# A masked attention without its empty quarter: 64x64 tiles for scores and values in a retention and feed-forward kernel

## The chip, the cores and the metric

The kernel runs on one NeuronCore of one Trainium2 chip. The metric is the time of one execution on the device, in microseconds (us). The profile is one execution of the program taken by the hardware profiler. TensorE (PE, with its weight loads PEld), VectorE (DVE), ScalarE (ACT), GpSimd (POOL) and SyncE (SP) are the engines; all loads and stores are issued on SP's queue.

## What is computed

For each batch and head, a decaying state collects the outer products of keys and values, and each query reads it. The result, all heads of a token side by side, goes through a feed-forward block with a rational function.

```python
batch, n_heads, seq, head_dim = (4, 8, 768, 64)
gamma = 1.0 - 2.0 ** (-5.0 - np.arange(H))
for t in range(S):
    state = gamma * state + outer(k[:, :, t], v[:, :, t])      # per batch and head, 64x64
    y[:, :, t] = scale * (q[:, :, t] @ state)
x = y.transpose(0, 2, 1, 3).reshape(B * S, H * D)              # 3072 tokens x 512
h = x @ w_in                                                   # 512 -> 2048
g = (a0 + a1*h + a2*h**2 + a3*h**3) / (1 + |b0|*|h| + |b1|*h**2 + 1e-6)
out = g @ w_out                                                # 2048 -> 512
```

## The kernel before

**Chunks.** Each sequence of 768 tokens is cut into C = 6 chunks of 128, so there are 24 chunks, numbered 0 to 23; chunk i is number i % 6 of its sequence. For a chunk the state of the tokens ahead is read (`recall`), and the tokens of the chunk itself attend to each other under a causal mask. All of this is fp32.

- `scores` (L220): k times q for all 8 heads into two PSUM banks `pa`. A head is h = 4a + 2r + j with a, r, j in 0, 1; r says in which half of the 128 partitions the 64 dimensions of the head lie in `qT` and `kT`. Each matmul has 64 rows, 128 keys and 128 queries, and the two values of r take the upper and the lower half of the array.
- `mask` (L231): VectorE multiplies each bank by the causal mask into `aT`, two instructions of 128x512.
- `outer` (L239): k times v over the 128 tokens, the new part of the state (`pk`), in the second half of bank `px[1]`. Not done for the last chunk of a sequence.
- `recall` (L252): state times q into `px`; 64 rows and 64 columns a matmul, so four fit in the array. Not done for the first chunk of a sequence.
- `values` (L266): v times `aT` over 128 keys for 128 queries, 64 columns a matmul, added into `px`.
- `update`, `x_out`: VectorE adds `pk` to the state, scales `px`, and splits the result into two fp32r parts `xh` and `xl` (ScalarE and VectorE). `scale_state` and `scale_v` put the decay on state and v and run on GpSimd.

**Feed-forward.** Four chunks make a block of 512 tokens; there are six blocks. For each block and each of 16 slices of the inner dimension `gemm_in` (12 matmuls of 128x512 fp32r, L355) writes a bank `ph`; ScalarE, GpSimd and VectorE work out the rational function (L366 to L395), and `gemm_out` (12 matmuls, L410) comes LAG = 3 slots later. A slot is one such slice.

**Order of the work.** The order on TensorE, VectorE, ScalarE, GpSimd and SP is that of the code: there is no scheduler. `opening` does chunks 0 to 3. Then `run` goes through 96 slots; the attention of chunk 4 and after is laid between the slots by the table `parts`: part 0 of a chunk is its scores and mask, part 1 the rest. In a slot with part 1 TensorE does gemm_in, then outer, recall, values, then gemm_out. The weights come as raw words and are decoded in the first 25 slots or so (`decode_read`, `decode_join`, `decode_split`, `decode_rest`); the banks that these use rotate with `pa` and `px`.

**Loads.** kT of a chunk is loaded two chunks ahead in part 0, and qT, v and k in part 1 (`load_rest`, L197). Chunks 2 and 3 land in buffers that the feed-forward uses later (`borrowed`, L180).

## Time and profile before

| | before |
|---|---|
| timed runs, median of 3 (lowest, highest) | 644.6 us (644.24, 645.17) |
| profiled execution, first to last instruction (span) | 642.4 us |
| TensorE busy | 620.0 us, 97% |
| VectorE, ScalarE, GpSimd busy | 460.1, 441.7, 334.1 us |
| matmuls | 3739 |
| mean DMA rate | 82 GB/s, 52.36 MB in all |

The page gives no time of its own for the profiled execution but its span; the timed runs are 2.2 us longer, which lies before the first and after the last instruction. A row of the views names the line of the code, the engine, the operation, what it writes and reads, its shape, and how many instructions stand in it; the time in square brackets is how long the engine sat idle ahead of it, and what ended that.

### The profile page before, as it was taken

How to read it: one execution, taken by the hardware profiler on the slowest of the kernel's cores; microseconds unless marked ns; L12 is line 12 of the kernel's file. 1: busy time of each engine (PE TensorE's matmuls, PEld its weight loads, DVE VectorE, ACT ScalarE, POOL GpSimd, SP SyncE). 2: the span in 40 equal slices, each digit the busy share in tenths (PEclk: the TensorE clock that was granted, in tenths of full speed). 3: DMA queues.
4: the chain of work that ended last, by engine and by line, in shares of the span. 5: the costliest groups of instructions: out<-in, count | busy, mean ns of one | idle time of the engine just before them, and what ended most of it. 6: DMA issues, size and time to landing. Idle time of an engine off the chain costs nothing.

```text
span 642.4 us, 10022 instructions
## 1 busy us (share of the span) xinstructions
PE 620.0 (97%) x3739; PEld 498.2 (78%) x3742; DVE 460.1 (72%) x731; ACT 441.7 (69%) x721; POOL 334.1 (52%) x288
## 2 busy tenths in 40 slices
PE   8777999999999999999999999999999999999997
PEld 5555778888877778788888878878888888888885
DVE  3788788888888666767676676667766766666664
ACT  2687889889885556566656575766666666777773
POOL 2566668887874434444544453535354434444442
PEclk9988999999999999999999999999999999999999
DMA  8984572001033222310110321001311000010001
GB/s 316 400 331 167 201 252 109 1 1 65 1 121 127 66 67 82 132 51 17 49 50 17 115 51 50 34 21 54 108 33 35 1 0 1 26 41 2 1 1 65
DMA packets 24384, 52.36 MB, mean 82 GB/s; under 512 B 3088, under 2 KB 3216, under 8 KB 24336
## 3 DMA queue, kind: packets, MB, share of 16 engines
q1 hardware_dynamic: 24336, 51.73, 23.4%
q8 instruction: 29, 0.48, 0.3%
q14 instruction: 19, 0.16, 0.1%
HBM read 43.33 MB, written 8.39 MB: 81 GB/s over the span
## 4 chain that ended last, share of the span: by engine, by line
PE 85%; DMA 4%; ACT 4%; DVE 3%; issue 2%; SPq 1%; POOL 0%; POOLq 0%; DVEq 0%; ACTq 0%
PE ph L355 38%; PE po L410 38%; PE px L271 3%; PE pa L226 3%; DMA v<-in_v 1%; PE px L260 1%; PE px L247 1%; DMA qT<-in_qT 1%; DMA k<-in_k 1%; DMA xdec_sb<-in_xdec 1%; ACT s L372 1%; SPq L192 1%; DVE o L428 1%; ACT t L128 1%; ACT q L366 1%
## 5 line engine op out<-in xcount | busy, mean ns | idle before, releaser
L373 POOL TENSOR_TENSOR q<-q,s 128x512 f32<-128x512 f32 x96 | 124.3, 1295 | 228.0 <-ACT s L372 217.9
L355 PE MATMUL ph<-xh,w 128*128 128x512 f32 (+2 forms) x776 | 210.3, 393 | 8.4 <-DVE p L389 4.8
L410 PE MATMUL po<-w,gh 128*128 128x512 f32 x768 | 200.2, 393 | 0.0
L355 PEld LDWEIGHTS ph<-xh,w 128*128 128x128 f32 x776 | 143.9, 188 | 41.5 <-DVE t L147 2.8
L410 PEld LDWEIGHTS po<-w,gh 128*128 128x128 f32 x768 | 142.9, 188 | 32.4 <-ACT p L374 1.5
L366 ACT ACTIVATE q<-ph 128x512 f32<-128x512 f32 x96 | 57.2, 596 | 118.6 <-PE ph L355 118.5
L378 DVE TENSOR_TENSOR p<-ph,p 128x512 f32<-128x512 f32 x96 | 66.2, 690 | 94.3 <-ACT p L374 94.3
L395 POOL TENSOR_TENSOR gl<-p,gh 128x512 fp32r<-128x512 f32 x96 | 124.3, 1295 | 8.9 <-ACT gh L394 3.6
L410 PE MATMUL po<-w,gl 128*128 128x512 f32 x384 | 110.5, 389 | 0.2 <-POOL gl L395 0.2
L387 DVE SCALAR_TENSOR_TENSOR q<-q,qcon,ph 128x512 f32<-128x512 f32 x96 | 71.4, 744 | 47.0 <-ACT ph L384 46.8
L355 PE MATMUL ph<-xl,w 128*128 128x512 f32 (+2 forms) x388 | 103.9, 390 | 0.0
L383 ACT ACTIVATE s<-q,qcon 128x512 f32<-128x512 f32 x96 | 69.4, 722 | 22.5 <-POOL q L373 22.5
L355 PEld LDWEIGHTS ph<-xl,w 128*128 128x128 f32 x388 | 72.8, 188 | 15.3
L410 PEld LDWEIGHTS po<-w,gl 128*128 128x128 f32 x384 | 72.1, 188 | 15.6 <-POOL gl L395 0.6
L379 DVE SCALAR_TENSOR_TENSOR p<-p,par_sb,ph 128x512 f32<-128x512 f32 x96 | 71.8, 748 | 3.4
L374 ACT ACTIVATE p<-ph,par_sb 128x512 f32<-128x512 f32 x96 | 73.1, 761 | 0.0
L388 DVE SCALAR_TENSOR_TENSOR ph<-p,par_sb,ph 128x512 f32<-128x512 f32 x96 | 72.0, 750 | 0.0
L394 ACT CAST gh<-p 128x512 fp32r<-128x512 f32 x96 | 58.8, 613 | 15.9 <-DVE p L389 15.9
L389 DVE SCALAR_TENSOR_TENSOR p<-q,ph 128x512 f32<-128x512 f32 x96 | 65.9, 687 | 3.3
L372 ACT ACTIVATE s<-q,babs 128x512 f32<-128x512 f32 x80 | 65.3, 817 | 2.7
L384 ACT ACTIVATE ph<-s 128x512 f32<-128x512 f32 x96 | 57.8, 602 | 10.0 <-DVE p L379 0.8
L210 POOL TENSOR_TENSOR v<-v,vdec_sb 128x512 f32<-128x512 f32 x24 | 25.0, 1044 | 43.9 <-DMA v<-in_v 43.9
(37 smaller groups left out, 446.2 us busy)
## 6 DMA issues: line engine op xcount, KB each, us to landing
raw<-in_w_in SPq DMA_DIRECT2D x16, 512.0 KB, 5.4
raw<-in_w_out SPq DMA_DIRECT2D x16, 512.0 KB, 7.4
kT<-in_kT SPq DMA_DIRECT2D x24, 256.0 KB, 2.8
qT<-in_qT SPq DMA_DIRECT2D x24, 256.0 KB, 3.0
v<-in_v SPq DMA_DIRECT2D x24, 256.0 KB, 3.5
out<-o SPq DMA_DIRECT2D x24, 256.0 KB, 2.2
k<-in_k SPq DMA_DIRECT2D x20, 256.0 KB, 3.7
half<-o SPq DMA_DIRECT2D x8, 256.0 KB, 2.2
```

Of the source, the lines that this page charges most:

```text
L355: nc.tensor.matmul(ph[:, t0:t1], w1[f][:, part, kt * P : (kt + 1) * P], x[:, kt, t0:t1], start=(i == 0), stop=(i == 3 * NP - 1),)
L372: nc.scalar.activation(s, q, AF.Identity, bias=babs[:, 0:1], scale=babs[:, 1:2])
L373: nc.gpsimd.tensor_mul(q, q, s)
L374: nc.scalar.activation(p, ph, AF.Identity, bias=par_sb[:, 2:3], scale=par_sb[:, 3:4])
L378: nc.vector.tensor_mul(p, ph, p)
L379: nc.vector.scalar_tensor_tensor(p, p, par_sb[:, 1:2], ph, ALU.add, ALU.mult)
L383: nc.scalar.activation(s, q, AF.Abs_reciprocal_sqrt, bias=qcon[:, 0:1])
L387: nc.vector.scalar_tensor_tensor(q, q, qcon[:, 0:1], ph, ALU.add, ALU.mult)
L388: nc.vector.scalar_tensor_tensor(ph, p, par_sb[:, 0:1], ph, ALU.add, ALU.mult)
L389: nc.vector.scalar_tensor_tensor(p, q, 2.0, ph, ALU.subtract, ALU.mult, reverse0=True)
L395: nc.gpsimd.tensor_sub(gl, p, gh.bitcast(F32))
L410: nc.tensor.matmul(o_tiles[n][tt], g_[:, tt * P : (tt + 1) * P], w2[f][:, part], start=(first and m == 0), stop=(last and m == 2),)
```

## The change

In a causal mask over 128 keys and 128 queries, the quarter of late keys (64 to 127) with early queries (0 to 63) is zero. The changed kernel leaves that quarter out.

- **Scores** are sixteen matmuls instead of eight, each with 64 rows and 64 keys: the early keys of a head with all 128 queries, its late keys with the 64 late queries. Each takes a quarter of the array (64x64). For half of the heads (a = 1) the halves of the partitions are exchanged in `qT` and `kT` (`crossed`), and for the heads with r = 1 early and late tokens are exchanged in `k` and `v` (`by_token`), so that all four quarters have work and two heads share 192 columns of a bank: 64 early queries of both, 64 late ones of each.
- **Mask**: two instructions of 128x384 instead of 128x512; the mask in memory has 192 columns instead of 128.
- **Values** come in two groups: `values_early` (64 early keys, 64 early queries, 64x64 tiles) and `values_late` (128 keys, 64 late queries, 128x64 tiles). Eight matmuls each.
- **Recall** keeps its eight matmuls; since q of the heads with a = 1 is exchanged, it reads these from a further load `q2T`, 128x256 (128 KB), for every chunk that is not the first of its sequence: 20 loads more on SP's queue.
- **Order**: in `run` outer now comes last, behind the late values; in `opening` it stays first.
- **Small things**: seven constants share one tile `small`, the zeros of the opening lie in a buffer of `o`, and the borrowed buffers have one shape.

TensorE at the scores of chunk 7, before (names: `pa` the banks written, `ph` and `po` the feed-forward's):

```order
L410 MATMUL po<-w,gh 128x512 x8
L410 MATMUL po<-w,gl 128x512 x4
L226 MATMUL pa<-qT,kT 128x128 x8
L355 MATMUL ph<-xh,w 128x512 x4
L355 MATMUL ph<-xl,w 128x512 x4
```

And after, the same place; 64x2x64 is a matmul of 128 queries that writes two separate blocks of 64 columns:

```order
L447 MATMUL po<-w,gl 128x512 x4
L254 MATMUL pa<-qT,kT 64x128
L254 MATMUL pa<-qT,kT 64x2x64
L254 MATMUL pa<-qT,kT 64x64 x4
L254 MATMUL pa<-qT,kT 64x2x64
L254 MATMUL pa<-qT,kT 64x128 x2
L254 MATMUL pa<-qT,kT 64x2x64
L254 MATMUL pa<-qT,kT 64x64 x4
L254 MATMUL pa<-qT,kT 64x2x64
L254 MATMUL pa<-qT,kT 64x128
L392 MATMUL ph<-xh,w 128x512 x4
```

Eight matmuls of 128 columns became eight of 128 and eight of 64, with half the keys each. Part 1 of the same chunk on TensorE, before (L247 outer, L260 recall, L271 values):

```order
L355 MATMUL ph<-xh,w 128x512 x4
L247 MATMUL px<-v,k 64x64 x8
L260 MATMUL px<-qT,state 64x128 x8
L271 MATMUL px<-aT,v 64x128 x8
L410 MATMUL po<-w,gh 128x512 x8
```

After (L287 recall, L297 early values, L308 late values, L274 outer):

```order
L392 MATMUL ph<-xh,w 128x512 x4
L287 MATMUL px<-qT,state 64x128 x4
L287 MATMUL px<-q2T,state 64x128 x4
L297 MATMUL px<-aT,v 64x64 x8
L308 MATMUL px<-aT,v 64x64 x8
L274 MATMUL px<-v,k 64x64 x8
L447 MATMUL po<-w,gh 128x512 x8
```

Outer moved from the first place to the last, and values became two groups of half the columns. SP's queue at part 1 of chunk 12, where the loads of chunk 14 stand behind the stores of a block, before:

```order
L434 DMA out<-o 128x512 x4
L192 DMA qT<-in_qT 128x512
L192 DMA v<-in_v 128x512
L192 DMA k<-in_k 128x512
L192 DMA kT<-in_kT 128x512
```

And after:

```order
L471 DMA out<-o 128x512 x4
L195 DMA qT<-in_qT 128x512
L195 DMA q2T<-in_q2T 128x256
L195 DMA v<-in_v 128x512
L195 DMA k<-in_k 128x512
L195 DMA kT<-in_kT 128x512
```

v and k now stand behind one more load. The core of the diff:

```diff
 def load_rest(i):
     load_part(i, "qT", qT, 1, [P, NP, P])
+    if i % C > 0:
+        load_part(i, "q2T", q2T, 4, [P, 2, P])
     load_part(i, "v", v, 3, [P, H, D])
...
 def scores(i):
-    for aj in range(NP):
-        for r in range(2):
-            rows = slice(r * D, (r + 1) * D)
-            nc.tensor.matmul(
-                pa[r][:, aj], st["kT"][rows, aj], st["qT"][rows, aj], start=True, stop=True
-            )
+    pa = [bank("pa")[:, : 6 * D].rearrange("p (j t) -> p j t", t=3 * D) for _ in range(2)]
+    for j in range(2):
+        for a in range(2):
+            whole, part = [], []
+            for s in range(2):
+                r = s ^ a
+                kt, qt = (st[n][half(s), 2 * a + j] for n in ("kT", "qT"))
+                to = pa[s][half(r), j, : 3 * D if a != s else 2 * D]
+                if a != s:
+                    to = to.rearrange("p (x t) -> p x t", t=D)[:, ::2]
+                    qt = qt.rearrange("p (x t) -> p x t", t=D)
+                whole.append((to, kt[:, :D], qt))
+                qt = st["qT"][half(s), 2 * a + j]
+                part.append((pa[s][half(1 - r), j, later(a, s)], kt[:, D:], qt[:, D:]))
+            for to, kt, qt in part + whole if a else whole + part:
+                nc.tensor.matmul(to, kt, qt, start=True, stop=True, skip_group_check=True)
...
+def values_early(i):
+    for a in range(2):
+        for j in range(2):
+            for r in range(2):
+                nc.tensor.matmul(
+                    st["px"][r][half(j), a * P : a * P + D],
+                    st["v"][half(r), 4 * a + 2 * r + j], st["aT", r ^ a][half(r), j, :D],
+                    start=(c == 0), stop=(c == 0), skip_group_check=True,
+                )
+def values_late(i):
+    for a in range(2):
+        for r in range(2):
+            for j in range(2):
+                nc.tensor.matmul(
+                    st["px"][r][half(j), a * P + D : (a + 1) * P],
+                    st["v"][:, 4 * a + 2 * r + j], st["aT", r ^ a][:, j, later(a, r ^ a)],
+                    start=(c == 0), stop=(c == 0 or a == 1), skip_group_check=True,
+                )
...
 if part == 1:
-    outer(chunk)
-    recall(chunk)
-    values(chunk)
+    recall(chunk)
+    values_early(chunk)
+    values_late(chunk)
+    outer(chunk)
```

## The prediction

> **What bounds the kernel now.** I read the page first, then the windows by stage, then TensorE's order of time inside one chunk, then the waits.

> ```profile
> PE 620.0 (97%) x3739; PEld 498.2 (78%) x3742; DVE 460.1 (72%) x731; ACT 441.7 (69%) x721; POOL 334.1 (52%) x288
> ...
> PE 85%; DMA 4%; ACT 4%; DVE 3%; issue 2%; SPq 1%; POOL 0%; POOLq 0%; DVEq 0%; ACTq 0%
> ```

> TensorE is busy for 97% of the span and is 85% of the chain that ended last. The windows (length, then busy time of each engine, the granted clock, the DMA share and GB/s) say where this holds:

> ```profile
> 0.00:24.00 24.00, 19.74 (x255) 13.17 (x258) 13.70 (x31) 8.69 (x17) 8.60 (x13) 1.00 0.92 342
> 24.00:57.50 33.50, 22.59 (x177) 17.35 (x173) 27.33 (x47) 27.08 (x47) 20.87 (x19) 0.91 0.76 289
> 57.50:95.00 37.50, 36.62 (x244) 29.42 (x243) 30.85 (x53) 29.81 (x53) 22.90 (x21) 0.99 0.66 222
> 245.00:540.00 295.00, 293.69 (x1801) 237.23 (x1800) 201.80 (x322) 190.32 (x304) 133.41 (x112) 1.00 0.16 49
> ```

> Up to 24 us the loads bound it (DMA share 0.92), up to 57.5 us VectorE and ScalarE with the decoding of the weights; behind that TensorE has under 1 us idle in 37.5 and 1.3 in 295. Chunks 0 to 3 lie in the first stretch, 4 and 5 in the second. So TensorE time counts for chunks 6 to 23, 18 of the 24.

> **The price of a pass.** Chunk 10 on TensorE, in order of time (start, busy us, group):

> ```profile
> 213.71 1.16 PE L226 MATMUL pa<-qT,kT 64*128 64x128 f32 x16
> 214.80 1.19 PE L355 MATMUL ph<-xh,w 128*128 128x512 f32 x4
> ...
> 217.75 0.69 PE L247 MATMUL px<-v,k 128*64 128x64 f32 x16
> 218.36 0.67 PE L260 MATMUL px<-qT,state 64*64 64x128 f32 x16
> 218.96 1.09 PE L271 MATMUL px<-aT,v 128*64 128x128 f32 x16
> 219.98 2.11 PE L410 MATMUL po<-w,gh 128*128 128x512 f32 x8
> ```

> Eight matmuls of the program stand as sixteen, so an fp32 matmul is two passes. From start to start the groups take: scores (L226) 1.09, outer (L247) 0.61, recall (L260) 0.60, values (L271) 1.02 us. Their medians:

> ```profile
> L247 PE MATMUL px<-v,k x320: 221/222/369, 7.6 to 507.9; 128*64 128x64 f32 x160
> L260 PE MATMUL px<-qT,state x320: 269/269/473, 12.9 to 533.4; 64*64 64x128 f32 x160
> L271 PE MATMUL px<-aT,v x384: 272/273/474, 8.7 to 534.4; 128*64 128x128 f32 x192
> ```

> A group's busy time less its last matmul is the time from first to last start: 1.09 - 0.27 = 0.82 us for values, 0.69 - 0.22 = 0.47 for outer. Both run two at a time, in the two column halves, so these are 7 steps each, and 64 columns more cost 0.35/7 = 0.05 a step. As much I put to the first weight load, which nothing covers: a step of 128 columns is (0.82 - 0.05)/7 = 0.11 us, one of 64 is 0.06. I take 0.1095 and 0.059. Over its 8 steps a group then has 0.14 (0.61 - 8 x 0.059) or 0.15 us (1.02 - 8 x 0.1095), for the change of the tile size. Recall has four tiles of 64x64 at work: 4 rounds of 0.1095 leave 0.16 of its 0.60, the same. With nothing put to the weight load the steps would be 0.117 and 0.067 and the change 0.08, and a middle chunk below would gain 0.25, not 0.31.

> **The group of part 1.** Middle chunks have all three groups, 2.23 us (217.75 to 219.98). Now recall and early values share the 64x64 size, late values and outer the 128x64 size: one tile change fewer, and the early keys of the late queries stay while the late keys of the early ones go. Recall 4 x 0.1095 = 0.44, early values 4 rounds of 64 columns 0.24, change 0.155, late values 8 x 0.059 = 0.47, outer 0.47, change 0.15: 1.92 us, 0.31 less. The first and the last chunk of a sequence:

> ```profile
> 232.41 0.67 PE L260 MATMUL px<-qT,state 64*64 64x128 f32 x16
> ...
> 234.03 0.50 PE L410 MATMUL po<-w,gh 128*128 128x512 f32 x1
> ```
> ```profile
> 252.36 0.69 PE L247 MATMUL px<-v,k 128*64 128x64 f32 x16
> ...
> 253.85 0.73 PE L410 MATMUL po<-w,gh 128*128 128x512 f32 x2
> ```

> Last (no outer): 1.62 before; 0.44 + 0.24 + 0.155 + 0.47 + 0.15 = 1.45 after, 0.17 less. First (no recall): 1.49 before, 0.24 + 0.155 + 0.47 + 0.47 + 0.15 = 1.48 after: it loses a quarter of its values and gains a tile change. Chunks 6 to 23 hold 12 middle, 3 last and 3 first ones: 12 x 0.31 + 3 x 0.17 + 3 x 0.01 = 4.3 us.

> **Scores.** Before, 8 steps of 128 columns in two row halves, 1.09 us. Now sixteen matmuls on four tiles: each tile gets long, short, long, short (or short first), 128 and 64 queries. No row shows unequal matmuls side by side; the bounds are recall's and outer's steps. If each tile runs its own list, a tile takes 2 x (2 x 0.1095 + 2 x 0.059) = 0.67, and with 0.155 the group is 0.83 us, 0.26 less. If matmuls may only start in program order, a tile waits for its turn behind a long one twice: the last starts at 0.56 and the group is 0.56 + 0.22 + 0.155 = 0.93, 0.16 less. I take 0.83, by this row, the first round of a recall:

> ```profile
> 188.42 0.34 PE L260 MATMUL px<-qT,state 64*64 64x128 f32 x4
> ```

> Four passes of 0.27 us or more lie within 0.34, so they started within 0.07, less than a step: the next tile's matmul did not wait for the second pass of the one ahead. [...]

> **Where the shorter scores do not count.** Waits of TensorE at part 1 that are not its own:

> ```profile
> 70.61 0.69 PE L247 MATMUL px<-v,k 128*64 128x64 f32 x16 [0.44 <-PE ph L355]
> ...
> 187.81 0.69 PE L247 MATMUL px<-v,k 128*64 128x64 f32 x16 [0.53 <-PE ph L355]
> ...
> 203.08 0.69 PE L247 MATMUL px<-v,k 128*64 128x64 f32 x16 [0.54 <-DVE aT L235]
> ```
> ```profile
> 69.83 0.69 DVE L147 SCALAR_TENSOR_TENSOR t<-raw,u 128x512 uint32<-128x512 uint32 x1
> ...
> 199.35 2.48 DVE L428 TENSOR_TENSOR o<-po,o 128x512 f32<-128x512 f32 x4
> 201.75 1.28 DVE L235 TENSOR_TENSOR aT<-pa,causal_sb 128x512 f32<-128x512 f32 x2
> ```

> At 70.61 the px bank came free with the decode that ended at 70.52; chunks 6, 7 and 8 (187.81) have this wait, and a shorter scores group only lengthens it. Chunk 9 (203.08) waits for its mask, which stood behind four adds. There the mask's own length counts: 1.28 us for two of 512 columns, against 0.75 for two of 256 here:

> ```profile
> 221.39 0.42 DVE L284 TENSOR_TENSOR state<-px,state 128x256 f32<-128x256 f32 x1
> 221.72 0.75 DVE L294 TENSOR_TENSOR px<-px,xdec_sb 128x256 f32<-128x256 f32 x2
> ```

> 384 columns lie halfway, 1.02: 0.26 gained once; elsewhere the mask is off the path. The first of these rows also says what outer's last place costs: VectorE takes up the state's sum at 221.39, 1.4 us after the group's end at 219.98, so it does not wait for outer.

> **The extra loads.** q2T, 128 KB, stands on SP's queue between qT and v, so v (then k, and later loads) is late, and GpSimd's scaling of v holds up its next product:

> ```profile
> 264.47 1.04 POOL L210 TENSOR_TENSOR v<-v,vdec_sb 128x512 f32<-128x512 f32 x1 [4.97 <-DMA v<-in_v]
> 265.48 1.28 POOL L373 TENSOR_TENSOR q<-q,s 128x512 f32<-128x512 f32 x1
> ```
> ```profile
> 270.44 0.74 PE L355 MATMUL ph<-xh,w 128*128 128x512 f32 x2 [1.11 <-DVE p L389]
> ```

> This chain ends in TensorE's 1.11 us at 270.44; its v (chunk 14) comes behind four stores. What 128 KB take goes by the fullest of the page's 40 slices:

> ```profile
> GB/s 316 400 331 167 201 252 109 1 1 65 1 121 127 66 67 82 132 51 17 49 50 17 115 51 50 34 21 54 108 33 35 1 0 1 26 41 2 1 1 65
> ```

> At 400 GB/s they are 0.33 us, so the wait grows by 0.33, and chunk 13's shorter scores, which stand ahead of that wait, are lost in it. Bounds: 0 (the loads before it are late anyway) to 1.8, which the issue ahead of v took once:

> ```profile
> 258.89 1.83 SPq L192 DMA_DIRECT2D qT<-in_qT  x1
> ```

> Chunk 22's v is the other one behind stores with a q2T:

> ```profile
> 466.43 1.04 POOL L210 TENSOR_TENSOR v<-v,vdec_sb 128x512 f32<-128x512 f32 x1 [3.01 <-DMA v<-in_v]
> ```
> ```profile
> 456.35 0.69 PE L247 MATMUL px<-v,k 128*64 128x64 f32 x16
> ```

> It comes 10 us behind its part 1, chunk 14's 12 (252.36 to 264.47), and TensorE has no gap after it; 0.33 us more is covered. At the other loads GpSimd idles afterwards.

> In the opening the q2T of chunks 1 to 3 and 32 KB of mask are 416 KB, 1.06 us at that rate, ahead of v of chunk 3. Its values move from 24.08 to about 25.1 us at their end:

> ```profile
> 23.06 1.09 PE L271 MATMUL px<-aT,v 128*64 128x128 f32 x16
> 24.08 0.97 PE L355 MATMUL ph<-xh,w 128*128 128x384 f32 x4
> ```
> ```profile
> 24.89 0.42 DVE L284 TENSOR_TENSOR state<-px,state 128x256 f32<-128x256 f32 x1
> ```

> VectorE takes them up at 24.89, so 0.8 of it was slack: with qT of chunk 3 late too, but shorter masks, I get 0.35 us, bounds 0 and 1.06. Chunk 5 gives it back: its recall and values took 2.96 us (54.53 to 57.49), at half clock,

> ```profile
> 54.53 1.13 PE L260 MATMUL px<-qT,state 64*64 64x128 f32 x14 [1.72 <-DVE t L147]
> ...
> 57.49 0.71 PE L410 MATMUL po<-w,gh 128*128 128x512 f32 x1
> ```

> and save 2 x 0.17. I set the opening at nothing. The constants in one tile and the zeros in a store's buffer move no instruction.

> **Sum.** Part 1: 4.3. Scores of 13 chunks (18 less 6, 7, 8, 9, 13) x 0.26 = 3.4. Mask of chunk 9: 0.26. Chunk 14's load: -0.33. Together 7.6 us. The profiled span of 642.4 becomes 634.8; the three timed runs have a median of 644.6, 2.2 us more than that span, so I forecast 637.0. A change of 0.2% (1.3 us) is about what can be told from none here.

> **Rivals.** (a) Starts in program order: scores save 0.16, 1.3 us less: 638.3. The first round of recall speaks against it.
> (b) The late v costs more: 1.8 us at chunk 14, and at chunk 22 some 0.7, where v would pass from 10 to 12 us after its part 1: 637.0 + 1.5 + 0.7 = 639.2. For it: the 1.83 us issue; against it: it fell once on these three loads.
> (c) A floor for the issue of passes over all tiles. No group before goes faster than recall's 0.44/16 = 0.027 us a pass; early values would need 0.015, scores 0.021. At 0.027 early values take 0.44, not 0.24, and scores 0.86 + 0.155 = 1.02. Middle chunks then save 0.11, last ones lose 0.03, first ones lose 0.19, scores save 0.07: 1.3 - 0.1 - 0.6 + 0.9 - 0.1 = 1.4 us, 643.2. Against it: the four starts above, at most 0.07/3 = 0.023 apart. [...]
> (d) Slower: unequal matmuls are dealt out in rounds, and each of the four rounds of scores empties the array, 0.155 us, before the next: 4 x (0.22 + 0.155) = 1.50 us, 0.41 more than before. Over 18 chunks that is 7.4, against 4.3 from part 1: 647.7. It decides from a scores group of 1.33 us on (4.3/18 = 0.24 above 1.09). Recall's equal rounds follow each other with no such gap, which speaks against it.

> **Chances.** Likeliest case 0.55, (a) 0.16, (b) 0.12, (c) 0.12, (d) 0.05. The range takes in the likeliest case with its bounds (all 18 scores counted and no late v: 1.7 us better), (a) and (b), and leaves out (c) and (d), 0.17: 635.0 to 640.5. Faster by over 0.2%: the first three and half of (c), 0.88; within: 0.07; slower: 0.05.

> **What would show it.** Right: scores start to start 0.83, the middle group 1.92, late values and outer with no gap between them, TensorE busy some 7 to 8 us less, 0.44 to 0.8 us waits ahead of part 1 in chunks 6 to 8 and under 0.3 in chunk 9. Scores of 0.93 would be (a), of 1.02 with early values at 0.44 (c), of over 1.3 (d); a gap of over 2 us after chunk 14's load (b). It would be wrong above all if short matmuls on four tiles cost more than recall's and outer's steps.

## The result and the profile after

The changed kernel takes 639.9 us (median of four runs, 639.1 to 641.4) against 644.4 us for before (four runs, with the profiled one); the ratio is 0.9926 (95% interval 0.9909 to 0.9943). The forecast was 637.0 us, in a range of 635.0 to 640.5. The profiled execution has a span of 638.0 us, where 634.8 was forecast. Two executions that ran several times slower throughout are left out of all figures: one of before, of 1564.6 us, timed beside e12, and the profiled one of e11, of 3420.8 us.

Two rows of its page, busy time by engine and the chain that ended last:

```profile
PE 611.7 (96%) x4506; PEld 494.4 (77%) x4510; DVE 452.9 (71%) x731; ACT 441.4 (69%) x721; POOL 334.2 (52%) x288
...
PE 67%; ACT 13%; DVE 11%; issue 5%; DMA 2%; POOL 1%; SPq 1%; POOLq 0%; DVEq 0%; ACTq 0%
```

TensorE is busy 8.3 us less, yet ScalarE and VectorE now hold 24% of the chain, where they held 7%. More than half of this lies between 80 and 200 us, where TensorE is busy for 119.3 of the 120 us (119.0 before): the chain runs beside a busy TensorE there, and shows no new limit. To see where time was gained and lost, cut both spans at the same places of the program, which are the first product of the first layer, the scores of chunk 6 and chunk 23's recall, and by the clock at 245 us. Windows of before, then of after (length, busy PE, PEld, DVE, ACT, POOL, granted clock, DMA share, GB/s):

```profile
0.00:24.08 24.08, 19.82 (x255) 13.17 (x258) 13.78 (x31) 8.69 (x17) 8.60 (x13) 1.00 0.92 343
24.08:66.07 41.99, 31.08 (x211) 24.23 (x209) 32.86 (x57) 32.85 (x58) 25.30 (x22) 0.92 0.72 269
66.07:245.00 178.93, 176.83 (x1045) 142.60 (x1045) 148.40 (x235) 140.54 (x237) 122.02 (x107) 1.00 0.27 90
245.00:532.97 287.97, 286.66 (x1746) 231.47 (x1744) 196.26 (x312) 185.83 (x296) 130.85 (x110) 1.00 0.16 50
```
```profile
0.00:26.11 26.11, 19.08 (x382) 12.66 (x386) 12.68 (x31) 8.63 (x17) 8.71 (x14) 0.93 0.94 340
26.11:69.45 43.34, 31.24 (x276) 24.91 (x273) 32.68 (x57) 32.83 (x58) 25.16 (x22) 0.88 0.72 266
69.45:245.00 175.55, 173.97 (x1250) 140.61 (x1249) 145.37 (x233) 139.78 (x236) 121.42 (x107) 1.00 0.28 96
245.00:528.55 283.55, 281.97 (x2105) 229.47 (x2101) 193.38 (x314) 186.44 (x298) 131.58 (x111) 1.00 0.18 55
```

From chunk 6's scores to chunk 23's recall before takes 466.90 us and after 459.10: **7.8 us gained**, and 7.6 was the forecast of the whole sum. Ahead of chunk 6's scores after is **3.4 us late** (69.45 against 66.07), 2.0 of them already at the first product, where the opening was set at nothing.

The gain is where it was forecast. Chunk 10 of after, on TensorE in order of time:

```profile
215.85 0.90 PE L254 MATMUL pa<-qT,kT 64*64 64x128 f32 x32
216.68 1.20 PE L392 MATMUL ph<-xh,w 128*128 128x512 f32 x4
...
219.62 0.45 PE L287 MATMUL px<-qT,state 64*64 64x128 f32 x8
219.89 0.40 PE L287 MATMUL px<-q2T,state 64*64 64x128 f32 x8
220.11 0.41 PE L297 MATMUL px<-aT,v 64*64 64x64 f32 x16
220.45 0.69 PE L308 MATMUL px<-aT,v 128*64 128x64 f32 x16
220.97 0.64 PE L274 MATMUL px<-v,k 128*64 128x64 f32 x16
221.53 2.11 PE L447 MATMUL po<-w,gh 128*128 128x512 f32 x8
```

Scores 0.83 us from start to start (1.09 before), part 1 1.91 (2.23 before). A last and a first chunk, 1.44 (1.62) and 1.48 us (1.49):

```profile
233.69 0.45 PE L287 MATMUL px<-qT,state 64*64 64x128 f32 x8
...
235.13 1.20 PE L447 MATMUL po<-w,gh 128*128 128x512 f32 x4
```
```profile
253.36 0.46 PE L297 MATMUL px<-aT,v 64*64 64x64 f32 x16
...
254.84 0.73 PE L447 MATMUL po<-w,gh 128*128 128x512 f32 x2
```

In the opening, chunk 2's scores and outer product, which came at 15.06 and 16.25 us before; then GpSimd's scaling of its v; then three windows:

```profile
15.48 0.89 PE L254 MATMUL pa<-qT,kT 64*64 64x128 f32 x31
16.71 0.32 PE L254 MATMUL pa<-qT,kT 64*64 64x128 f32 x1 [0.34 <-issue]
18.30 0.93 PE L274 MATMUL px<-v,k 128*64 128x64 f32 x16 [1.26 <-DVE px L329]
```
```profile
17.20 1.04 POOL L218 TENSOR_TENSOR v<-v,small 128x512 f32<-128x512 f32 x1 [3.97 <-DMA v<-in_v]
```
```profile
52.70:56.10 3.40, 0.40 (x2) 0.19 (x2) 2.38 (x4) 3.27 (x7) 2.98 (x3) 1.00 0.00 1
56.10:59.50 3.40, 2.60 (x47) 2.37 (x47) 3.30 (x5) 1.84 (x4) 1.28 (x1) 0.50 0.25 47
59.50:62.93 3.43, 3.43 (x9) 2.75 (x9) 2.69 (x6) 3.40 (x8) 2.96 (x3) 0.50 0.80 265
```

The 1.26 us at 18.30 is put down to VectorE, but the outer product reads v, whose scaling ends at 18.2; that v landed 2.05 us later than before. The stop of 0.34 us ahead of it ("issue") is over by then, so it is the late v that holds the outer product up here. And behind TensorE's waits at 52 to 57 us the clock is halved twice in a row, where before it was halved once (54.5 to 58.0); the second time it falls on the second layer's first product.

### The profile page after: what moved, and what is told of

It reads as the page before. It is cut to its first block, busy times and chain, and to the rows that moved or that the text cites. A ratio compares the mean times of both kernels' runs of the same rounds, so it can differ in the third digit from the quotient of the medians.

```text
span 638.0 us, 11577 instructions
## 1 busy us (share of the span) xinstructions
PE 611.7 (96%) x4506; PEld 494.4 (77%) x4510; DVE 452.9 (71%) x731; ACT 441.4 (69%) x721; POOL 334.2 (52%) x288
## 3 DMA queue, kind: packets, MB, share of 16 engines
q1 hardware_dynamic: 27216, 54.38, 25.1%
## 4 chain that ended last, share of the span: by engine, by line
PE 67%; ACT 13%; DVE 11%; issue 5%; DMA 2%; POOL 1%; SPq 1%; POOLq 0%; DVEq 0%; ACTq 0%
PE po L447 30%; PE ph L392 30%; ACT t L130 3%; ACT s L420 2%; ACT ph L421 2%; DVE q L424 2%; PE pa L254 2%; DVE p L426 2%; DVE ph L425 2%; PE px L308 2%; DMA v<-in_v 2%; PE px L287 2%; PE px L274 1%; ACT u L138 1%; ACT s L409 1%
## 5 line engine op out<-in xcount | busy, mean ns | idle before, releaser
L410 POOL TENSOR_TENSOR q<-q,s 128x512 f32<-128x512 f32 x96 | 124.4, 1296 | 224.1 <-ACT s L409 215.4
L424 DVE SCALAR_TENSOR_TENSOR q<-q,small,ph 128x512 f32<-128x512 f32 x96 | 71.4, 744 | 47.3 <-ACT ph L421 47.2
L420 ACT ACTIVATE s<-q,small 128x512 f32<-128x512 f32 x96 | 69.4, 723 | 22.7 <-POOL q L410 22.7
L416 DVE SCALAR_TENSOR_TENSOR p<-p,small,ph 128x512 f32<-128x512 f32 x96 | 71.8, 748 | 3.4
L411 ACT ACTIVATE p<-ph,small 128x512 f32<-128x512 f32 x96 | 73.2, 762 | 0.0
L425 DVE SCALAR_TENSOR_TENSOR ph<-p,small,ph 128x512 f32<-128x512 f32 x96 | 72.0, 750 | 0.0
L409 ACT ACTIVATE s<-q,small 128x512 f32<-128x512 f32 x80 | 65.3, 816 | 2.7
L218 POOL TENSOR_TENSOR v<-v,small 128x512 f32<-128x512 f32 x24 | 25.0, 1044 | 41.8 <-DMA v<-in_v 40.1
```

Of the source, the lines that this page charges most:

```text
L409: nc.scalar.activation(s, q, AF.Identity, bias=babs[:, 0:1], scale=babs[:, 1:2])
L410: nc.gpsimd.tensor_mul(q, q, s)
L411: nc.scalar.activation(p, ph, AF.Identity, bias=par_sb[:, 2:3], scale=par_sb[:, 3:4])
L416: nc.vector.scalar_tensor_tensor(p, p, par_sb[:, 1:2], ph, ALU.add, ALU.mult)
L420: nc.scalar.activation(s, q, AF.Abs_reciprocal_sqrt, bias=qcon[:, 0:1])
L424: nc.vector.scalar_tensor_tensor(q, q, qcon[:, 0:1], ph, ALU.add, ALU.mult)
```

## The experiments

**Is it the loads? (e1, e2, e3)** First the changed kernel again (e1). In e2 the q2T loads of chunks 1 to 5 are left out:

```diff
-        if i % C > 0:
+        if i % C > 0 and i >= SPB + 2:
             load_part(i, "q2T", q2T, 4, [P, 2, P])
...
-    qt = st["q2T"][half(r), j] if a else st["qT"][half(r), j]
+    qt = st["q2T"][half(r), j] if a and "q2T" in st else st["qT"][half(r), 2 * a + j]
```

> The changed kernel once more, as the measure for the others of this set. The first traces say: behind chunk 6's scores it gains 7.8 us (7.6 forecast), ahead of them it loses 3.4 us. Theory A (the late q2T loads leave TensorE idle in the opening, and the clock is halved once more for it): the loss returns in each run, 639.5 to 641.5 us, and half-clock windows stand near 18 to 22 and 56 to 63 us. Theory B (the windows fall by chance, whatever the kernel): the time scatters over 636.5 to 641 us, and a profile shows other windows than the first.

Measured: 639.2 us (638.6 to 640.1), ratio to before 0.9906 (0.9886 to 0.9926). Chunk 6's scores start at 69.44 us again, and from there to chunk 23's recall (527.92) it gains 8.4 us. The half clock of 56 us is there (55.6 to 62.4), the one of 18.6 us stands elsewhere (7.8 to 14.7): the loss returns, the places of the windows only in part. TensorE's rows of chunk 2 have no stop in the scores this time:

```profile
17.37 0.90 PE L254 MATMUL pa<-qT,kT 64*64 64x128 f32 x32 [0.20 <-DMA qT<-in_qT]
19.42 0.69 PE L274 MATMUL px<-v,k 128*64 128x64 f32 x16 [1.14 <-POOL v L218]
```

The outer product is 3.2 us later than before's (16.25) all the same. The rows above wait for the loads of qT and v.

> No q2T is loaded for chunks 1 to 5; their recall reads the same rows of qT for the four exchanged heads, so that the instructions stay and these heads' recall is not the reference's. Theory A: v of chunk 2 lands 1 us or more earlier, the window near 18 to 22 us is gone, chunk 6's scores start within 1.5 us of before's 66.07 us, and the time is 2 to 3 us under the changed kernel's, 637 to 638 us. Rival (the loss comes from the changed matmul groups or masks in the opening, not from the loads): chunk 6's scores stay 3 us late, and the time stays within 0.7 us of the changed kernel's.

Measured: 637.2 us (635.8 to 639.8), ratio 0.9879 (0.9848 to 0.9910), which overlaps e1's. In the profiled run, the slowest of the four, v of chunk 2 lands 0.7 us earlier than after's, at 16.44, and chunk 6's scores still start at 69.53. Theory A would not have that, though the time, 2.0 us under e1's, is the one it gave (637 to 638), so the run does not decide between the two. TensorE's rows of chunk 2, then its weight loads, show why the profile is late without q2T:

```profile
17.83 0.89 PE L254 MATMUL pa<-qT,kT 64*64 64x128 f32 x31
19.94 0.32 PE L254 MATMUL pa<-qT,kT 64*64 64x128 f32 x1 [1.22 <-issue]
20.19 0.69 PE L274 MATMUL px<-v,k 128*64 128x64 f32 x16
```
```profile
17.83 0.75 PEld L254 LDWEIGHTS pa<-qT,kT 64*64 64x64 f32 x31
19.94 0.13 PEld L254 LDWEIGHTS pa<-qT,kT 64*64 64x64 f32 x1 [1.36 <-issue]
```

Weight loads and matmuls both stop ahead of the last pass of the scores, and nothing is awaited ("issue"). It is the stop of 16.71 us above, but longer. Neither theory had it, and e12 takes it up.

In e3 the kernel before gets the loads alone:

```diff
         load_part(i, "qT", qT, 1, [P, NP, P])
+        if i < NSTEP and i % C > 0:
+            nc.sync.dma_start(out=st["q2T"], in_=qT[i // C, i % C][:, 2:])
         load_part(i, "v", v, 3, [P, H, D])
```

> The kernel before with one thing added: the second half of each qT is loaded once more behind qT, into a tile that nothing reads (the zeros lie in a store's buffer to make room). Loads like the changed kernel's, with everything else as before. Theory A: the opening loses 2 to 3.5 us against before, 646.5 to 648 us. Theory B (chance windows) or loads that are hidden: within 0.7 us of before, 644 to 645 us.

Measured: 647.6 us (646.9 to 649.4), ratio 1.0041 (1.0027 to 1.0056): **2.8 us slower** by loads alone, between theory A's 2 and 3.5. In the profile 2.2 of them stand ahead of chunk 6's scores (68.28), with two halved windows (54.5 to 61.3) where before has one, and 0.8 in chunk 14's late v (1.11 before):

```profile
273.52 1.20 PE L363 MATMUL ph<-xh,w 128*128 128x512 f32 x4 [1.91 <-DVE p L397]
```

**What does a change of tile size cost? (e4)**

```diff
+                outer(chunk, early=True)
                 recall(chunk)
                 values_early(chunk)
                 values_late(chunk)
-                outer(chunk)
```

> The changed kernel with the outer product ahead of recall again in chunks 4 to 23: one change of tile size more in 12 middle and 3 first chunks of the stretch that TensorE bounds. If a change costs the 0.14 to 0.16 us of the prediction: a middle chunk's group of part 1 takes 2.06 instead of 1.91 us, and the time is 15 x 0.155 = 2.3 us above the changed kernel's, 642 us. Rival (a change of size costs nothing by itself, and the gain is from the shorter matmuls alone): 1.91 us a group, and no difference in time. In chunks 7 to 9 the wait for the px bank then stands ahead of the group and not inside it, which may give back up to 0.5 us.

Measured: 640.6 us (639.7 to 642.1), ratio 0.9930 (0.9903 to 0.9957): 1.4 us over e1, within the intervals. The profile is sharper:

```profile
219.38 0.69 PE L274 MATMUL px<-v,k 128*64 128x64 f32 x16
...
220.83 0.69 PE L308 MATMUL px<-aT,v 128*64 128x64 f32 x16
221.44 0.73 PE L447 MATMUL po<-w,gh 128*128 128x512 f32 x2
```

2.06 us, 0.15 more than after's 1.91: each change of size costs 0.15 us. From chunk 6's scores (68.58) to the end of the span (638.6) it takes 570.0 us, where e1 takes 567.9 (69.44 to 637.3): 2.1 us more, where 2.3 was forecast. Nothing is given back in chunks 7 to 9: from chunk 6's scores to chunk 10's it takes 147.0 us, e1 146.4, and four changes make 0.6. The rival, no cost, falls.

**Can the loss be mended? (e5 to e8)** e5 moves `load_again(i)`, the load of q2T, behind v and k; e6 issues the second layer's first product ahead of chunk 5's recall; e8 is both; e7 puts `fill(6)` ahead of chunk 2's outer product.

```diff
         load_part(i, "qT", qT, 1, [P, NP, P])
-        load_again(i)
         load_part(i, "v", v, 3, [P, H, D])
         if i % C < C - 1:
             load_part(i, "k", kk, 2, [P, H, D])
+        load_again(i)
```
```diff
+            if k == LAG:
+                gemm_out(*order[0], *g.pop(0))
             if part == 1:
                 steps[chunk]["px"] = px_banks(chunk)
...
-                gemm_out(n, f, *g.pop(k - LAG))
+                if k > LAG:
+                    gemm_out(n, f, *g.pop(k - LAG))
```

> The changed kernel with q2T loaded behind v and k instead of ahead of v. Theory A: v of chunk 2 lands near before's 15.1 us, TensorE's wait ahead of chunk 2's outer product is gone with the half clock behind it, and the 0.43 us wait near 470 us (chunk 22's v) is gone too: 1.5 to 3 us under the changed kernel's, 637 to 638.5 us. Rival (the mere amount of the loads delays the opening, whatever their order): the same time as the changed kernel.

Measured: 637.5 us (636.3 to 640.0), ratio 0.9899 (0.9870 to 0.9928), 1.8 us under e1 with overlapping intervals. Its profile is again the slowest run; the loads of chunk 2 came late by themselves there (qT at 17.45 us), and the stop in the scores is 1.34 us. What it does show: no wait near 470 us.

> The changed kernel with the first product of the second layer issued ahead of chunk 5's recall, where TensorE waits 2.0 and 2.0 us (near 52.5 to 56.9 us), instead of behind its values. If the product's operands are there by then, one of the two waits is filled: 2 us less, and if the half clock of 56.1 to 62.9 us goes with it 1.5 us more, 636.5 to 638 us. Rival (VectorE and ScalarE, which decode the weights there, set the time of the next product whatever TensorE does first): within 0.5 us of the changed kernel.

Measured: 636.1 us (635.7 to 636.6), ratio 0.9872 (0.9856 to 0.9888): 3.1 us under e1, apart from it. The half clock of 56 to 63 us is gone (granted clock 1.00 from 49.27 to 62.93, where after has 0.50 from 56.10 on).

> The changed kernel with six matmuls on zeros ahead of chunk 2's outer product, where TensorE waits for v (16.9 to 18.3 us); they take 1.3 us at full clock and end before v is there. Nothing else moves. If the half clock at 18.6 to 22.0 us comes from TensorE's idle time, it is gone: some 1 to 1.5 us of it come back, 638.5 us. Rival (late loads alone cost the time, and the halved clock there costs nothing, because chunk 3's loads are late anyway): within 0.5 us of the changed kernel.

Measured: 638.5 us (637.3 to 639.1), ratio 0.9907 (0.9885 to 0.9929). Inconclusive: the stop in chunk 2's scores lasted 2.19 us in this run, to 18.94, so the zeros came behind it and put the outer product off to 20.59. The premise, that TensorE waits there for v alone, was wrong.

> q2T behind v and k, and the second layer's first product ahead of chunk 5's recall, together. If the two losses are apart, the gains add up: 3 to 5 us under the changed kernel's, 635 to 637 us. Rival (both mend one and the same delay): no more than the better of the two.

Measured: 634.8 us (633.6 to 635.4), ratio 0.9850 (0.9832 to 0.9868): 4.4 us under e1, 1.3 under e6. In the profiles 1.2 us of the difference stand in one place, the product behind the scores of chunk 21, which waits for VectorE, and that for GpSimd, held up by chunk 22's v. In after, in e6 and in e8:

```profile
470.27 1.19 PE L392 MATMUL ph<-xh,w 128*128 128x512 f32 x4 [0.43 <-DVE p L426]
```
```profile
467.07 1.20 PE L392 MATMUL ph<-xh,w 128*128 128x512 f32 x4 [1.39 <-DVE p L426]
```
```profile
465.38 1.20 PE L392 MATMUL ph<-xh,w 128*128 128x512 f32 x4 [0.15 <-DVE p L426]
```

**Was e6's gain the change's loss? (e9, e10)** e9 is e6's edit on the kernel before; e10 is e6 with e2's edit.

> The kernel before with the second layer's first product issued ahead of chunk 5's part 1, as in e6. It waits there too, 2.27 and 1.72 us, and its half clock of 54.5 to 58.0 us lies beside. Reading 1 (e6's 3.1 us were a loss that the change had brought, by a second half-clock window at 59.5 to 62.9 us): before gains clearly less, 0 to 1.5 us, 643 to 644.5 us. Reading 2 (the wait was there all along, and filling it is worth the same with or without the change): 2.5 to 3.5 us less, 641.5 us, and then e6 says nothing of where the forecast's 3 us went.

Measured: 641.6 us (641.1 to 643.0), ratio 0.9959 (0.9945 to 0.9973): **2.8 us**. Reading 2: that wait was there all along. e6 is an improvement, not an explanation, and the second halved window is no part of the shortfall that shows: without it e6 is 5.5 us under e9, as after was 4.6 and e1 5.6 under before.

> e6 without q2T for chunks 1 to 5 (recall reads qT for the exchanged heads there, so these heads' recall is not the reference's). The stretch at 52 to 63 us, where a half clock came and went, is filled as in e6, so that what is left is the price of the opening's loads. Theory A (late loads pass through the whole opening): 1 to 2.5 us under e6, 634 to 635 us. Rival (late loads cost nothing but the half clock that e6 has already taken away): the same as e6, 636 us.

Measured: 635.9 us (634.5 to 637.3), ratio 0.9861 (0.9841 to 0.9881): as e6, the rival's time. But the profile shows v of chunk 2 late without any q2T (17.82) and the stop in the scores (0.77 us), so it does not say that late loads cost nothing.

**The wait of 2.9 us behind chunk 4's scores (e11)**, filled with zeros:

```diff
+            if k == 1:
+                idle = early_bank("idle", "po2")
+                for _ in range(10):
+                    nc.tensor.matmul(idle, zeros[:, :P], zeros, start=True, stop=True)
```

> e8 with ten matmuls on zeros in TensorE's wait of 2.9 us behind chunk 4's scores (31.6 to 34.5 us), which the half clock of 33.4 to 40.2 us follows. If that half clock holds up the end, 1 to 2 us less than e8, 633 us. Rival (behind it VectorE and ScalarE set the pace: the next product waits 1.76 us for VectorE at 43.77 us): the half clock goes, the wait at 43.8 us grows, and the time stays at e8's 634.8 us.

Measured: 634.8 us over four runs (633.7 to 637.3), ratio 0.9855 (0.9836 to 0.9875), e8's time, as the rival had it. The only profile of e11 is that of the execution left out, with a span of 3419.1 us, so what became of the half clock was not seen.

**The stop in the scores (e12).** The profile's page says what queue 8 brings (packets, MB, share of the DMA engines), for before and after:

```profile
q8 instruction: 29, 0.48, 0.3%
```
```profile
q8 instruction: 35, 0.57, 0.4%
```

After has 4506 + 4510 rows of TensorE (matmuls and weight loads), before 3739 + 3742: 258 rows a packet in both, so I take these packets to be TensorE's code, 16 KB each. In e4, where the stop is longest, the first of them goes over at 16.26 to 17.36 us, and the last pass follows at 18.71:

```profile
15.59 0.89 PE L254 MATMUL pa<-qT,kT 64*64 64x128 f32 x31
18.71 0.32 PE L254 MATMUL pa<-qT,kT 64*64 64x128 f32 x1 [2.23 <-issue]
```

In the eight traces with this stop it stands at the same place, near TensorE's 442nd row, and ends 1.2 to 1.5 us behind the packet's landing. In e1 the packet had landed at 15.74, ahead of these scores (17.37). There a stop of 0.34 us stands some 254 rows further, in chunk 3's recall at 25.36, 1.4 us behind the landing of the next packet (23.96). With the old attention the 442nd row comes only at 21.7 to 22.7 us (before, e3, e9), 4.5 us or more behind the packet.

e12 issues 112 instructions more ahead of chunk 0's scores, so that whatever hangs on the count comes so much earlier in the program:

```diff
         fill(FILL[0])
+        for _ in range(FILL[2]):
+            nc.tensor.matmul(idle[:D, :D], zeros[:, :D], zeros[:, :D], start=True, stop=True)
...
-FILL = (10, 2)
+FILL = (5, 2, 61)
```

> e8 with 5 of the opening's 10 first matmuls on zeros replaced by 61 small ones (64 x 64), so that TensorE issues 112 instructions more ahead of chunk 0's scores, in about the same time. In nine of the nine traces with the new attention seen so far but one, TensorE's weight loads and matmuls both stop at the last pass of chunk 2's scores for 0.3 to 2.4 us with nothing awaited, and go on 1.2 to 1.5 us behind a 16 KB packet of queue 8's instructions; the old attention never shows it. Theory C (TensorE runs out of loaded instructions there: the new attention has 64 a scores group where the old has 32, and the packet stands in line with the loads): the stop moves with the count, 112 instructions ahead, to chunk 1's values, where the packet has been asked for at 6 us and has landed by then; chunk 2's scores take 0.9 us in one piece, and the time is 0.5 to 1.2 us under e8's, 633.6 to 634.3 us. Rival (the stop belongs to these scores: a bank, a port or the loads): it stays at their last pass, and the time stays at 634.8 us.

Measured: the first packet goes over at 10.70 us (16.29 in e8; when a packet is asked for stands in no view, so the 6 us expected were an estimate), and chunk 2's scores are one piece:

```profile
17.17 0.90 PE L254 MATMUL pa<-qT,kT 64*64 64x128 f32 x32 [0.84 <-DMA qT<-in_qT]
18.87 0.69 PE L274 MATMUL px<-v,k 128*64 128x64 f32 x16 [0.80 <-POOL v L218]
19.48 0.45 PE L287 MATMUL px<-qT,state 64*64 64x128 f32 x8
20.39 0.45 PE L287 MATMUL px<-q2T,state 64*64 64x128 f32 x8 [0.46 <-DMA q2T<-in_q2T]
```

No stop is left in chunks 0 to 3; every wait behind chunk 1's scores is for a load. With the places of the other stops this is for theory C: the stop belongs to the count of instructions, not to these scores. Time: 634.2 us (633.2 to 635.6), ratio 0.9836 (0.9821 to 0.9850). That is 0.6 under e8, as theory C said, but within the intervals, so the price of the stop is not shown by a time. Nor by the trace: this profile is of the slowest of the five runs, chunk 3's v landed at 23.60 in it (21.61 in e8), and the first product comes at 27.52, 1.3 us later than in e8 (26.25). e8 and e12 beat both kernels.

## Why the prediction was right, and where it failed

- **Pass prices and part 1**: right. 0.32, 0.18 and 0.02 us less (the last from unrounded times) for middle, last and first chunks, where 0.31, 0.17 and 0.01 were forecast. The 0.155 us for a change of tile size measured 0.15 (e4).
- **Scores**: right, 0.83 us. Rivals (a), 0.93, (c), 1.02, and (d), 1.50, fall with it; early values, 16 passes in 0.34 us, 0.021 a pass, say the same of (c)'s floor of 0.027 over all tiles. That each tile runs its own list, as the 0.83 assumed, agrees with the order of starts. In chunk 7 passes of the early values (L297) start ahead of the last passes of recall (L287), which stand ahead of them in the program:

```profile
88.47 0.37 PE L287 MATMUL px<-q2T,state 64*64 64x128 f32 x4
88.58 0.27 PE L297 MATMUL px<-aT,v 64*64 64x64 f32 x2
88.67 0.28 PE L287 MATMUL px<-q2T,state 64*64 64x128 f32 x3
```

So starts in program order, which (a) supposes, were not what these tiles showed. And the first four passes of chunk 10's early values start within 0.02 us (220.110 to 220.130). Before's trace had that already, in chunk 10's recall (218.362 to 218.382), so (c) deserved less than its 0.12.
- **Mask of chunk 9**: right, 1.01 us for two against 1.28:

```profile
204.49 1.01 DVE L261 TENSOR_TENSOR aT<-pa,causal_sb 128x384 f32<-128x384 f32 x2
```

- **Chunks 6 to 9**: 1.24 us gained up to chunk 10's scores, by 0.31 x 3 + 0.26 + 0.01 = 1.20. Recall now stands in the wait for the px bank; the sum did not suffer. The waits there were 0.40, 0.29 and 0.37 us in chunks 6 to 8, less than the 0.44 to 0.8 given as a sign, and 0.17 in chunk 9, under 0.3 as forecast.
- **Chunk 14's v**: too dear. With the shorter scores its wait was to grow by 0.6, from 1.11 to 1.7 us, and is 0.95; in the other runs of the changed attention with q2T ahead of v it was 0 to 0.90. e3 had 1.91, so this load simply varies.
- **Chunk 22's v, "covered"**: wrong. 0.43 us in after, 0.61, 1.51, 0.44, 1.39 and 1.01 in e1, e2, e7, e6 and e10, none in e4. Rival (b) had said 0.7 here.
- **A wait with no term**: 0.32 us ahead of the first layer's product at 238.46, for `xh` from ScalarE. It stands in all ten traces of the changed attention at 0.32 or 0.33 us, and in none of the three with the old.
- **7.8 for 7.6** is in part luck: chunk 14's wait came 0.75 us shorter than forecast, and chunk 22's and the one for `xh` add as much. In e1 the same stretch gains 8.4.
- **The opening, "at nothing"**: the step that failed, by 3.4 us in the profile. The loads were put at 0.35 us, to be given back in chunk 5. The bounds, 0 to 1.06, came from the bytes at 400 GB/s; v of chunk 2 alone landed 2.05 us late. The loads by themselves cost 2.8 us in all on the kernel before (e3). A second thing had no term at all: twice the instructions in a scores group (64 for 32), which, by theory C, run TensorE out of code while the packet stands among the loads. The stop shows without q2T (e2), late loads without the stop in chunk 2 (e1, e12). In e1 chunk 6's scores are as late as in after, and chunk 2's outer product waits for its v with no stop ahead of it, so the loss does not need the stop. That a stop makes up for late loads where they are gone would explain why taking one of the two away moved the time by no more than the intervals, but this is argued, not shown.

So the time came within the range by the forecast gain, less an opening that was priced wrongly. That the range held this loss is luck: it reached up to 640.5 for rivals (a) and (b), not for the opening. With q2T behind v and the 112 instructions more, e12 is 7.4 us under e9, the kernel before with the same product ahead. That is near the 7.6 of the sum, though each side is uncertain by about 1 us and e9 has not e12's other edits. Not settled: how the opening's loss divides between loads and code (no run had neither), and how much is a disturbance of single executions; e9 runs before's own program up to 51 us and had its first product 1.3 us later (25.37 against 24.08); its profile, like those of e2, e5, e6 and e12, is of the slowest of its runs.

## What to carry to other kernels

Where one engine is busy without a gap, a change of matmul shapes can be priced from the steps and shape changes of the trace to some tenths of a microsecond over hundreds: here 7.8 us were gained over 467, for 7.6. Where the DMA queues are full, price a load by who stands behind it in line, not by its bytes, and put it behind what is needed sooner: the loads that were put at 0.35 us in the opening cost 2.2 ahead of chunk 6's scores in e3, at a DMA share of 0.94 up to 26 us. Count instructions there too: the smaller tiles made 64 of 32 in a scores group here, and the page counts the code's packets on the same 16 DMA engines as the data (0.4% of their time in after, 25.1% for the data). What a stop for code costs, no time here shows.
